# Two key/query buffers instead of four, and the second gate product ahead of the scores

## The chip, the cores and the metric

One core of one Trainium2 chip runs the whole kernel. The metric is the device time of one execution in microseconds (us). A profiled execution shows what TensorE (PE, with its weight loads as PEld), VectorE (DVE), ScalarE (ACT), GpSimd (POOL) and SyncE (SP, which only issues transfers) did and when.

## The reference, cut to what matters

A gated linear attention over 4 batches of 8 heads, 768 steps, head size 40, and behind it a mixture of 8 experts with the best two per token. The attention keeps a matrix `C` and a vector `n` per head and step:

```python
for t in range(S):
    m_new = np.maximum(f_gate[:, :, t] + m, i_gate[:, :, t])
    f_stab = np.exp(f_gate[:, :, t] + m - m_new)
    i_stab = np.exp(i_gate[:, :, t] - m_new)
    C = f_stab * C + i_stab * outer(v, k)
    n = f_stab * n + i_stab * k
    y[:, :, t] = sigmoid(o_gate) * (C @ q) / max(abs(n @ q), 1)
```

The expert part turns the 3072 tokens of 320 features into logits, picks two experts per token, and adds `relu(x @ w1[e]) @ w2[e]` with the two weights.

## The kernel before

The attention is cut into 24 units: two pairs of batches times 12 chunks of 64 steps, each unit with all 8 heads. Inside a unit the steps are handled as a 64 x 64 product per head. A unit u passes through these steps:

- `load_unit(u)` (line 154): keys and queries (`"k"`, four transfers into `QK[u % 4]`, line 159) and values with output gates (`"v"`, two transfers into `VKS[u % 4]`, lines 162 and 163), issued on SP.
- `s_part(u)` (line 333): the scores, 32 small products of keys and queries (line 342), and for all units but the first of a pair 8 products that copy the queries below them (line 339), into PSUM tile `s`, which has two buffers.
- `e_part(u, p)` (line 312): for each half p one matmul of the gate terms `LE` and `RE` into PSUM tile `e` (line 318), which has one buffer, and ScalarE's exponential of it into `W[u]` (line 321).
- `k_part(u)` and `p_part(u)`: VectorE multiplies keys by gate factors (`kd`, line 350) and scores by gate factors (`p`, line 356, or line 360 for the first unit of a pair).
- `c_part(u)`: products into PSUM tile `st` (line 370), the state for the next unit; ScalarE copies it beside the values of u + 1 (line 373).
- `o_part(u)` (line 379): the output products. `f_part(u)`: VectorE divides (lines 384 to 390), POOL multiplies by the gate (`xr`, line 391). `sig_part(u)`: three ScalarE steps make the sigmoid of the output gate.
- `t_part`, `tc_part`, `l_part`, `lc_part`: the output is transposed (line 402), and the router's logits are computed (line 422).

The order on each engine is that of the program text; there is no scheduler. Iteration i of the loop (line 792) emits: transfers for i + 3; `k_part` and `p_part` of i + 1; `c_part` and `o_part` of i; the first half of `e_part(i + 2)`; `f_part(i)`; logits and transposes of i - 1; `s_part(i + 2)`; ScalarE's `sig_part(i + 1)`; the second half of `e_part(i + 2)`; and then pieces of the router's work (`fill`, `act`), which VectorE, ScalarE and POOL do in between. The router ends in bursts of matmuls (line 442) on one-hot tiles `ob` that VectorE makes (line 615).

Rows of `QK` that no transfer fills are cleared once by `blank(i)` (lines 176 to 178), on VectorE or POOL. `keys(i)` (line 246) does the same for `VK`, on POOL. `gate_math` and `gate_move` make the gate terms on VectorE and bring them to `LE` and `RE`.

The pools `att` (with `QK` and `VKS`) and `wk` are closed behind the loop (line 924). The pool `m2` (line 931) of the expert phase takes their place in SBUF: first `RAW2` (10 KB per partition), a filler of `PAD` = 544 words, and then `HH`, the hidden layer, whose first write is at line 992. A tile there waits for the last use of the tiles that it lies over.

Of the kernel before, what the change touches and what calls it, by code (L numbers as in the profile page):

```python
# [7 lines left out]
F32 = mybir.dt.float32  # L8
# [8 lines left out]
B, H, S, D = 4, 8, 768, 40  # L17
# [44 lines left out]
def build(ctx, tc, qk, vk, fi, noise, wgn, w1, w2, cst, ce, out):  # L62
# [39 lines left out]
    HL = gates.tile([64, 2, S], FR, name="hl")  # L102
    es = ExitStack()
    att = es.enter_context(tc.tile_pool(name="att", bufs=1))
    QK = [att.tile([128, 2, H, L], F32, name=f"qk{i}") for i in range(4)]

    VKS = [att.tile([128, 2, VW], F32, name=f"vk{i}") for i in range(4)]
    VK = [[t[:, p, 0:648] for p in range(2)] for t in VKS]
# [45 lines left out]
    def load_unit(u, what="kv", q=None):  # L154
        pr, c = divmod(u, NCH)
        if "k" in what:
            for n in (slice(0, 32), slice(32, D)):
                for p in range(2):
                    (q or SP).dma_start(QK[u % 4][64 * p + n.start:64 * p + n.stop], qk[pr, c, p, n])
        if "v" in what:  # L160
            flat = VKS[u % 4].rearrange("p x c -> p (x c)")
            SP.dma_start(flat[0:64, 0:VW], vk[pr, c, 0])
            SP.dma_start(flat[64:128, 648:648 + VW], vk[pr, c, 1])
# [12 lines left out]
    def blank(i, q):  # L176
        q.memset(QK[i][32:64], 0.0)
        q.memset(QK[i][96:128], 0.0)

# [12 lines left out]
    def run(steps):  # L192
        for _ in steps:
            pass

    def gate_math(t0, t1):
        f, i = fit[:, 0, t0:t1], fit[:, 1, t0:t1]
        n = t1 - t0
        V.tensor_tensor_scan(mt[:, t0 + 1:t1 + 1], f, i, mt[:, t0:t0 + 1], OP.add, OP.max)
        yield  # L200
        gt = gts[t0 // 128 % 2][:, 0:n]
        V.tensor_add(gt, f, mt[:, t0:t1])
        yield
        V.tensor_sub(gt, gt, mt[:, t0 + 1:t1 + 1])
        if t0 == 0:
            V.memset(gt[:, 0:1], 0.0)
        yield
        ag = ags[t0 // 128 % 2][:, :, 0:n]
        V.tensor_tensor_scan(ag[:, 1, :], rmt[:, 0:n], gt, 0.0, OP.mult, OP.add)
        yield  # L210
        V.tensor_sub(ag[:, 0, :], i, mt[:, t0 + 1:t1 + 1])
        yield
        V.tensor_sub(ag[:, 0, :], ag[:, 0, :], ag[:, 1, :])
        yield

        V.tensor_copy(HL[:, :, t0:t1], ag)
        yield
        V.scalar_tensor_tensor(HL[:, :, t0:t1], HL[:, :, t0:t1].bitcast(F32), cet[0:64, E_SG:E_SG + 1], ag, op0=OP.mult, op1=OP.add)
        yield
# [3 lines left out]
    def gate_move(kk, q=(SP, SP)):  # L223
        pr, k = divmod(kk, GB)
        j = kk % 2
        src = HL[32 * pr:32 * pr + 32, :, k * GC * L:(k + 1) * GC * L].bitcast(F32)
        q[0].dma_start(LE[j][64:96, :, 64:128].bitcast(F32), src[:, 0].rearrange("r (c t) -> r c t", c=GC))
        q[1].dma_start(RE[j][96:98].bitcast(F32), src[:, 1])

    def operands(j, p, eng=None):  # L230
        if p is None:
            A.activation(LE[j][0:KE], cet[0:KE, None, E_L:E_L + 192].to_broadcast([KE, GC, 192]), AF.Copy)
        else:
            A.activation(RE[j][0:64, p].rearrange("r h (c t) -> r h c t", c=GC),
                         cet[0:64, None, None, 0:L].to_broadcast([64, H, GC, L]), AF.Copy)

    def heads(j, p, eng):
        o, i = RE[j][64:96, p], cet[64:96, E_H:E_H + H, None].to_broadcast([32, H, GC * L])
        x = cet[64:96, E_P + p:E_P + p + 1]
        if eng is A:  # L240
            A.activation(o, i, AF.Copy, scale=x)
        else:
            V.tensor_scalar(o, i, x, None, op0=OP.mult)


    def keys(i):
        P.memset(VK[i][1][32:64, 0:328], 0.0)
        P.memset(VK[i][0][96:128, 328:648], 0.0)
        P.tensor_copy(VK[i][0][64:104, 328:648].rearrange("p (h d) -> p h d", h=H), ident[64:104, None, 64:104].to_broadcast([40, H, D]))
        P.tensor_copy(VK[i][1][0:64, 328:648].rearrange("p (h d) -> p h d", h=H), ident[0:64, None, 0:D].to_broadcast([64, H, D]))  # L250
# [7 lines left out]
    heads(0, 0, A)  # L258
    heads(0, 1, A)
    load_unit(1, "v")  # L260
    blank(2, P)
    for i in range(2):
        keys(i)
    load_unit(2, "k")
    operands(1, None, A)
    operands(1, 0, A)
    run(gate_math(GC * L, 256))
    gate_move(1)
    heads(1, 0, V)
    gates2 = (s for t0 in (256, 384, 512, 640) for s in gate_math(t0, t0 + 128))  # L270

    def gate_steps(n):
        for _ in range(n):
            next(gates2, None)

    gate_steps(4)
    blank(3, P)
    for i in range(2, 4):
        keys(i)
    load_unit(2, "v")  # L280
    load_unit(3, "k")
    SP.dma_start(fit[:, :, 384:], fi[:, :, 384:])
    SP.dma_start(wgt, wgn)
    def constants():
        P.memset(W1L[0:64, 2].bitcast(F32), 0.0)
        P.memset(zrow, 0.0)
# [44 lines left out]
        SQ[u] = psum.tile([128, 2, 512], F32, name="s", bufs=2).rearrange("p x (h t) -> p x h t", h=H)  # L331

    def s_part(u):
        q = QK[u % 4]
        for h in range(H):
            if whole(u) and h % 4 == 0:
                for p in range(2):
                    r = qrow[p]
                    T.matmul(SQ[u][:, p][r][:, h:h + 4, :], ident[r, r], q[r, 0, h:h + 4, :], start=True, stop=True)
            for p in range(2):  # L340
                r = qrow[p]
                T.matmul(SQ[u][:, p][half[p], h, :], q[r, 1, h, :], q[r, 0, h, :], start=True, stop=True)  # L342
# [102 lines left out]
    def bc_part(t, b, late=False):  # L445
        if b:
            s = late or rt.tile([128, NE * TC], F32, name="share", bufs=2)
            if late:
                V.tensor_add(TBL, TBL, t[:, LGC + 24:LGC + 24 + NE * TC])
            else:  # L450
                A.activation(s, t[:, LGC + 24:LGC + 24 + NE * TC], AF.Copy)
                P.tensor_add(TBL, TBL, s)
            done[0] += len(b[0]) // 2
# [234 lines left out]
    def warm(n):  # L688
        wp = psum.tile([128, 512], F32, name="o")
        for _ in range(n):  # L690
            T.matmul(wp, wz[:, 0:128], wz, start=True, stop=True)
# [3 lines left out]
    s_room(1)  # L695
    s_part(0)
    warm(WARM2)
    e_part(0, first=True)
    s_part(1)
    heads(1, 1, A)  # L700
    e_part(1, first=True)
    operands(1, 1, A)
# [89 lines left out]
    while i < NU - LEAD:  # L792
        unit[0] = i
        spent[0] = 0.0
        while sent:
            SP.dma_start(*sent.pop())
        if 1 <= i and i + 3 < NU:
            load_unit(i + 3)
        if i:
            keep_rows(i - 1)  # L800
        if i % 2 == 0 and i and i // 2 + 2 < 2 * GB:
            gate_move(i // 2 + 2, (P, P) if i < XV else (SP, SP))

        if W1LD <= i < W1LD + 12 and i % 2 == 0:
            j = (i - W1LD) // 2
            piece_w1(0, 512 * (j // 3), j % 3)
        if i == W2AT:
            early_w2(0, 2)
        if i == 3:
            SP.dma_start(cs[:, C_TRI:], cst[:, C_TRI:])  # L810
        if i == 4:
            SP.dma_start(nzt, noise)
        if not begun and done[0] >= E0U[0]:
            decode(0, E0S[1] // 128)
            spent[0] += 0.6
            begun = 1
        if begun and late < len(tiles(0, 0)):
            gather(0, 0, tiles(0, 0)[late:late + 2])
            late += 2
            begun = 2  # L820
        if i == 6:
            constants()
            A.activation(tri, cs[:, C_TRI:C_TRI + 128], AF.Copy)
            A.activation(ones, cs[:, C_ONE:C_ONE + 128], AF.Copy)
            A.activation(iob, cs[:, C_N:C_N + 128], AF.Copy)
        k_part(i + 1)
        p_part(i + 1)
        fill(0.2, False)
        s_room(i + 2)
        c_part(i)  # L830
        o_room(i)
        o_part(i)
        e_part(i + LEAD, (0,))
        if i == 0:
            sig_part(0)
        f_part(i, lambda: fill(0.15, False))
        if i < 2:
            gate_steps(4)
        if i == 0:
            gate_move(2, (P, P))  # L840
        t = l_part(i)
        w = r_part(t)
        b = None if w else b_part(t)
        if i:
            t_part(i - 1)
            tc_part(i - 1)
        lc_part(i, t, w)
        bc_part(t, b)
        s_part(i + 2)
        act()  # L850
        if i:
            sig_part(i + 1)
        e_part(i + LEAD, (1,))
        if i == 0:
            sig_part(1)
        route(i)
        fill((SHARE if i < NU - 3 else 0.8) - spent[0])
        if W1AT <= i < W1AT + 12 and i % 2 == 0:
            next(pre1)
        act()  # L860
        if 0 < i < 7:
            gate_steps(4)
        if 6 <= i < 13:
            P.memset(XG[:, i - 6], 0.0)
        i += 1
# [482 lines left out]
```

## Time and profile before

| what | us |
|---|---|
| three runs | 524.8, 528.34, 535.03 |
| their median | 528.34 |
| the profiled execution | 522.65 |
| its span, first to last instruction | 520.9 |
| mean granted TensorE clock in it | 0.985 of full |

The profiled execution is shorter than the three runs shown. Where the text reads places in the trace, times are us from the start of the span.

### The profile page before, as it was taken

What the parts mean: (1) busy time and instruction counts of PE and PEld (TensorE: products, weight loads), DVE (VectorE), ACT (ScalarE), POOL (GpSimd) and SP (SyncE); (2) the same over time, 40 slices, a digit from 0 to 9 for tenths busy, and PEclk for the clock granted to TensorE, in tenths of its full rate; (3) what the DMA queues carried; (4) which work ended last, traced back from release to release, by engine and by line L of the source; (5) the groups of instructions that cost most, each with busy time, mean ns of one, the idle gap of its engine ahead of it and who ended that gap; (6) DMA issues with size and microseconds to landing.
All of it is one profiled execution on the core that took longest, in us unless ns stands there. A gap on an engine that the chain in (4) does not pass through costs nothing.

```text
span 520.9 us, 13365 instructions
## 1 busy us (share of the span) xinstructions
PE 504.6 (97%) x5130; PEld 473.3 (91%) x5130; DVE 341.3 (66%) x905; ACT 248.7 (48%) x594; POOL 243.3 (47%) x321
## 2 busy tenths in 40 slices
PE   8899999999999999999999999999999999999993
PEld 3788888888889988999999999999999999999993
DVE  6899998986997576763865484377548347546310
ACT  5788879978523255441542354054335325515300
POOL 7545686864543846055415614550562254151033
PEclk9799999999989999999999999999999999999998
DMA  5889999986655848079229516832951683272033
GB/s 153 201 217 243 246 242 248 223 235 207 216 195 165 202 57 213 5 163 234 68 53 274 112 28 139 229 91 48 263 99 51 138 221 88 60 169 26 2 40 41
DMA packets 48955, 76.89 MB, mean 148 GB/s; under 512 B 10645, under 2 KB 37980, under 8 KB 48884
## 3 DMA queue, kind: packets, MB, share of 16 engines
q1 hardware_dynamic: 35668, 52.19, 36.3%
q0 software_dynamic: 11616, 20.57, 20.7%
q10 hardware_dynamic: 1600, 3.21, 2.0%
q8 instruction: 42, 0.69, 0.6%
q14 instruction: 29, 0.24, 0.2%
HBM read 52.42 MB, written 17.40 MB: 134 GB/s over the span
## 4 chain that ended last, share of the span: by engine, by line
PE 66%; DMA 13%; DVE 11%; ACT 3%; issue 2%; POOL 2%; SPq 1%; POOLq 0%; DVEq 0%; ACTq 0%
PE s L981 16%; DMA y_out<-y,tok 9%; PE e L981 8%; PE o L1009 4%; PE o L1008 4%; PE o L1007 4%; PE st L1008 4%; PE st L1009 4%; PE st L1007 4%; PE o L379 4%; PE e L318 3%; PE s L342 2%; DVE hlo L993 2%; PE st L370 2%; DMA qk<-qk_in 2%
## 5 line engine op out<-in xcount | busy, mean ns | idle before, releaser
L1035 POOL DMA_INDIRECT y_out<-y,tok x53 | 87.2, 1645 | 184.8 <-DVE y L1025 182.0
L992 ACT ACTIVATE hh<-s 128x384 fp32r<-128x384 f32 (+3 forms) x91 | 42.6, 470 | 83.8 <-PE s L981 82.7
L981 PE MATMUL s<-xh,w1h 128*128 128x384 f32 (+6 forms) x273 | 76.8, 337 | 0.1
L750 POOL DMA_INDIRECT xg<-rows,tok x53 | 57.3, 1082 | 24.6 <-issue 15.5
L993 DVE SCALAR_TENSOR_TENSOR hlo<-s,hh 128x384 fp32r<-128x384 f32 (+3 forms) x91 | 47.6, 523 | 24.9 <-ACT hh L992 24.3
L981 PE MATMUL s<-xh,w1l 128*128 128x384 f32 (+6 forms) x273 | 61.7, 334 | 0.0
L1009 PE MATMUL o<-w2h,hlo 128*128 128x320 f32 x184 | 56.9, 309 | 0.7 <-DVE hlo L993 0.7
L1008 PE MATMUL o<-w2l,hh 128*128 128x320 f32 x184 | 56.8, 309 | 0.0
L1007 PE MATMUL o<-w2h,hh 128*128 128x320 f32 x184 | 56.3, 306 | 0.2 <-ACT hh L992 0.2
L1009 PE MATMUL st<-w2h,hlo 128*128 128x320 f32 x168 | 51.9, 309 | 0.0
L1008 PE MATMUL st<-w2l,hh 128*128 128x320 f32 x168 | 51.8, 308 | 0.0
L1007 PE MATMUL st<-w2h,hh 128*128 128x320 f32 x168 | 51.2, 305 | 0.0
L981 PEld LDWEIGHTS s<-xh,w1h 128*128 128x128 f32 x273 | 49.2, 188 | 1.5 <-ACT xh L782 0.4
L981 PEld LDWEIGHTS s<-xh,w1l 128*128 128x128 f32 x273 | 47.7, 188 | 1.1 <-DVE xh L784 0.2
L981 PE MATMUL s<-xl,w1h 128*128 128x384 f32 (+6 forms) x182 | 46.1, 334 | 0.3 <-DVE xl L783 0.3
L992 ACT ACTIVATE hh<-e 128x384 fp32r<-128x384 f32 (+3 forms) x45 | 21.3, 473 | 49.3 <-PE e L981 49.3
L981 PE MATMUL e<-xh,w1h 128*128 128x384 f32 (+6 forms) x135 | 38.6, 340 | 0.6 <-DVE hlo L993 0.3
L1025 DVE TENSOR_SCALAR y<-o,gw 128x320 f32<-128x320 f32 x22 | 12.1, 550 | 39.9 <-PE o L1009 39.9
L391 POOL TENSOR_TENSOR xr<-tm,vk 128x320 f32<-128x320 f32 x24 | 21.1, 879 | 34.7 <-DVE tm L390 13.6
L1025 DVE TENSOR_SCALAR y<-st,gw 128x320 f32<-128x320 f32 x20 | 11.0, 550 | 39.3 <-PE st L1009 39.3
L1009 PEld LDWEIGHTS o<-w2h,hlo 128*128 128x128 f32 x184 | 34.5, 188 | 0.9 <-DVE hlo L993 0.9
L1007 PEld LDWEIGHTS o<-w2h,hh 128*128 128x128 f32 x184 | 34.5, 188 | 0.6 <-ACT hh L992 0.4
(237 smaller groups left out, 1290.7 us busy)
## 6 DMA issues: line engine op xcount, KB each, us to landing
vk<-vk_in SPq DMA_DIRECT2D x48, 242.0 KB
raw<-w_in SPq DMA_DIRECT2D x6, 1280.0 KB
raw<-w_in SPq DMA_DIRECT2D x6, 1024.0 KB
qk<-qk_in SPq DMA_DIRECT2D x46, 128.0 KB
y_out<-zrow SPq DMA_DIRECT2D x15, 320.0 KB
raw<-w_in SPq DMA_DIRECT2D x16, 256.0 KB
rows<-xr POOLq DMA_DIRECT2D x23, 160.0 KB, 4.3
xt__2801<-xb SPq DMA_DIRECT2D x40, 72.0 KB
```

The lines of the kernel that those rows point to most:

```text
L318: T.matmul(ps, LE[j][0:KE, c, 64 - 64 * p:192 - 64 * p], RE[j][0:KE, p, :, c * L:c * L + L], start=True, stop=True)
L379: T.matmul(OQ[u][half[p], h, :], PP[u][n, p, h, :], VK[u % 4][p][n, h * 41:h * 41 + 41], start=True, stop=True)
L391: P.tensor_mul(XR[u], tm.rearrange("p h d -> p (h d)"), SG[u % 4])
L750: P.indirect_dma_start(out=XG[0:rows_of(e, t), t], out_offset=None, in_=XD[0:n], in_offset=bass.IndirectOffsetOnAxis(ap=token(e, t), axis= ...
L981: T.matmul(ps[:, 0:n], l, r, start=i == 0, stop=i == len(ops) - 1)
L992: A.activation(hi, x, AF.Relu)
L993: V.scalar_tensor_tensor(lo, x, 0.0, hi.bitcast(F32), op0=OP.max, op1=OP.subtract)
L1007: T.matmul(ps, HH[:, j, c], W2H[:, j], start=j == 0, stop=False)
L1008: T.matmul(ps, HH[:, j, c], W2L[:, j], start=False, stop=False)
L1009: T.matmul(ps, HLO[:, j, c], W2H[:, j], start=False, stop=j == 7)
L1025: V.tensor_scalar(y[0:n], ps[0:n], GW[e][0:n, t:t + 1], None, op0=OP.mult)
L1035: st = P.indirect_dma_start(out=out, out_offset=bass.IndirectOffsetOnAxis(ap=token(e, t), axis=0), in_=y[0:n], in_offset=None, compute_op= ...
```

## The change

`QK` has two buffers instead of four. The two clears of buffers 2 and 3 go. In the loop, the head of iteration i loads only the values of unit i + 3; the keys and queries of unit i + 4 are asked for behind `s_part(i + 2)`, which is the last reader of the buffer that they go into. Ahead of the loop, part of the preparation (gate terms of the second pair of chunks, `keys(2)` and `keys(3)`, loads of units 2 and 3) now stands in the text behind `s_part(0)` and the warm-up matmuls, and the load of unit 3's keys behind `s_part(1)`. From iteration 2 on, the second half of `e_part(i + 2)` stands ahead of `s_part(i + 2)`, and so ahead of `act()` and `sig_part(i + 1)`. In iterations 0 and 1 the order of these is what it was.

```diff
--- before.py
+++ after.py
@@ -102,7 +102,7 @@
     HL = gates.tile([64, 2, S], FR, name="hl")
     es = ExitStack()
     att = es.enter_context(tc.tile_pool(name="att", bufs=1))
-    QK = [att.tile([128, 2, H, L], F32, name=f"qk{i}") for i in range(4)]
+    QK = [att.tile([128, 2, H, L], F32, name=f"qk{i}") for i in range(2)]
 
     VKS = [att.tile([128, 2, VW], F32, name=f"vk{i}") for i in range(4)]
     VK = [[t[:, p, 0:648] for p in range(2)] for t in VKS]
@@ -156,7 +156,7 @@
         if "k" in what:
             for n in (slice(0, 32), slice(32, D)):
                 for p in range(2):
-                    (q or SP).dma_start(QK[u % 4][64 * p + n.start:64 * p + n.stop], qk[pr, c, p, n])
+                    (q or SP).dma_start(QK[u % 2][64 * p + n.start:64 * p + n.stop], qk[pr, c, p, n])
         if "v" in what:
             flat = VKS[u % 4].rearrange("p x c -> p (x c)")
             SP.dma_start(flat[0:64, 0:VW], vk[pr, c, 0])
@@ -258,29 +258,8 @@
     heads(0, 0, A)
     heads(0, 1, A)
     load_unit(1, "v")
-    blank(2, P)
     for i in range(2):
         keys(i)
-    load_unit(2, "k")
-    operands(1, None, A)
-    operands(1, 0, A)
-    run(gate_math(GC * L, 256))
-    gate_move(1)
-    heads(1, 0, V)
-    gates2 = (s for t0 in (256, 384, 512, 640) for s in gate_math(t0, t0 + 128))
-
-    def gate_steps(n):
-        for _ in range(n):
-            next(gates2, None)
-
-    gate_steps(4)
-    blank(3, P)
-    for i in range(2, 4):
-        keys(i)
-    load_unit(2, "v")
-    load_unit(3, "k")
-    SP.dma_start(fit[:, :, 384:], fi[:, :, 384:])
-    SP.dma_start(wgt, wgn)
     def constants():
         P.memset(W1L[0:64, 2].bitcast(F32), 0.0)
         P.memset(zrow, 0.0)
@@ -331,7 +310,7 @@
         SQ[u] = psum.tile([128, 2, 512], F32, name="s", bufs=2).rearrange("p x (h t) -> p x h t", h=H)
 
     def s_part(u):
-        q = QK[u % 4]
+        q = QK[u % 2]
         for h in range(H):
             if whole(u) and h % 4 == 0:
                 for p in range(2):
@@ -695,8 +674,27 @@
     s_room(1)
     s_part(0)
     warm(WARM2)
+    load_unit(2, "k")
+    operands(1, None, A)
+    operands(1, 0, A)
+    run(gate_math(GC * L, 256))
+    gate_move(1)
+    heads(1, 0, V)
+    gates2 = (s for t0 in (256, 384, 512, 640) for s in gate_math(t0, t0 + 128))
+
+    def gate_steps(n):
+        for _ in range(n):
+            next(gates2, None)
+
+    gate_steps(4)
+    for i in range(2, 4):
+        keys(i)
+    load_unit(2, "v")
     e_part(0, first=True)
     s_part(1)
+    load_unit(3, "k")
+    SP.dma_start(fit[:, :, 384:], fi[:, :, 384:])
+    SP.dma_start(wgt, wgn)
     heads(1, 1, A)
     e_part(1, first=True)
     operands(1, 1, A)
@@ -795,7 +793,7 @@
         while sent:
             SP.dma_start(*sent.pop())
         if 1 <= i and i + 3 < NU:
-            load_unit(i + 3)
+            load_unit(i + 3, "v")
         if i:
             keep_rows(i - 1)
         if i % 2 == 0 and i and i // 2 + 2 < 2 * GB:
@@ -846,13 +844,18 @@
             tc_part(i - 1)
         lc_part(i, t, w)
         bc_part(t, b)
+        if i > 1:
+            e_part(i + LEAD, (1,))
         s_part(i + 2)
+        if i + 4 < NU:
+            load_unit(i + 4, "k")
         act()
-        if i:
+        if i == 1:
+            sig_part(2)
+        if i < 2:
+            e_part(i + LEAD, (1,))
+        if i != 1:
             sig_part(i + 1)
-        e_part(i + LEAD, (1,))
-        if i == 0:
-            sig_part(1)
         route(i)
         fill((SHARE if i < NU - 3 else 0.8) - spent[0])
         if W1AT <= i < W1AT + 12 and i % 2 == 0:
```

## Rows read from the trace of the kernel before

**Rows 1.** The page, busy time of the engines: us, share of the span, instructions.
```profile
PE 504.6 (97%) x5130; PEld 473.3 (91%) x5130; DVE 341.3 (66%) x905; ACT 248.7 (48%) x594; POOL 243.3 (47%) x321
```

**Rows 2.** Stretches: length, busy (count) of PE, PEld, DVE, ACT, POOL, clock, DMA, GB/s.
```profile
17.36:25.50 8.14, 8.14 (x139) 6.96 (x140) 6.13 (x13) 5.28 (x12) 3.02 (x6) 0.58 0.95 223
...
22.58:126.06 103.48, 101.80 (x2464) 87.98 (x2464) 90.07 (x233) 87.22 (x215) 66.81 (x104) 0.99 0.94 240
```

**Rows 3.** Chain that ended last, one iteration: start, length in us, what, instructions merged.
```profile
36.97 0.74 PE st L370 x32
...
38.65 0.43 PE e L318
...
40.02 0.21 PE s L339
...
41.12 0.43 PE e L318
41.55 0.75 PE st L370 x32
```

**Rows 4.** Timeline, SP's key issues; PE's gate products that follow scores 4 and 14.
```profile
28.41 2.27 SPq L159 DMA_DIRECT2D qk<-qk_in  x4
...
77.31 2.61 SPq L159 DMA_DIRECT2D qk<-qk_in  x4
...
31.40 0.50 PE L318 MATMUL e<-re,le 98*128 98x512 f32 x1
...
78.99 0.51 PE L318 MATMUL e<-re,le 98*128 98x512 f32 x1
```

**Rows 5.** The chain again: transfers of keys, from issue to landing.
```profile
4.23 2.98 DMA qk<-qk_in
...
50.02 6.82 DMA qk<-qk_in
```

**Rows 6.** Timeline, ScalarE's exponentials of two iterations, and PE's scores at 58.56.
```profile
39.11 0.60 ACT L321 ACTIVATE w<-e 128x512 f32<-128x512 f32 x1 [0.30 <-PE e L318]
...
41.89 0.58 ACT L321 ACTIVATE w<-e 128x512 f32<-128x512 f32 x1
...
58.00 0.58 ACT L321 ACTIVATE w<-e 128x512 f32<-128x512 f32 x1
...
58.56 0.43 PE L339 MATMUL s<-qk,cs 64*64 64x256 f32 x2
```

**Rows 7.** Waits in total: us, times, longest; then who waited for instructions on `qk`.
```profile
DVE kd L350 <- ACT w L321: 5.1, 5, 2.4
...
  PEld s L339: 0.5, 3
```

**Rows 8.** Timeline, the two bursts of rank matmuls, and one wait of VectorE.
```profile
76.47 1.14 PE L442 MATMUL xt<-oa,ob 128*128 128x56 bf16 x12
...
85.35 0.82 DVE L350 TENSOR_TENSOR kd<-vk,w 128x640 f32<-128x640 f32 x1 [1.30 <-ACT w L321]
...
105.41 0.91 PE L442 MATMUL xt<-oa,ob 128*128 128x56 bf16 x12
```

**Rows 9.** Timeline, the start: a clear on POOL, the cast twice, PE's first o.
```profile
11.14 0.95 POOL L178 MEMSET qk<- 32x1024 f32 x1
11.21 1.02 DVE L216 CAST hl<-xg 64x256 fp32r<-64x256 f32 x1
...
17.36 1.92 PE L379 MATMUL o<-vk,p 64*64 64x41 f32 x30 [0.36 <-DVE p L360]
...
28.67 0.28 DVE L216 CAST hl<-xg 64x256 fp32r<-64x256 f32 x1
```

**Rows 10.** Timeline, where the expert phase begins.
```profile
132.07 0.49 ACT L992 ACTIVATE hh<-s 128x384 fp32r<-128x384 f32 x1 [1.00 <-issue]
133.01 0.87 POOL L391 TENSOR_TENSOR xr<-tm,vk 128x320 f32<-128x320 f32 x1 [3.81 <-ACT lg L471]
...
134.67 0.54 DVE L993 SCALAR_TENSOR_TENSOR hlo<-s,hh 128x384 fp32r<-128x384 f32 x1
```

## What the change will do

> **What bounds the kernel now.** I read the page first: TensorE (PE) is busy 97% of the span, VectorE 66%, the rest under half [rows 1]. A busy matrix engine says little of stages with other limits, so the table by stretches comes next. The change touches only the attention loop and what stands ahead of it, so I cut out the stretch from iteration 1's first `st` product to the first transpose of the expert phase: 103.48 us, in which PE is busy 101.80, ScalarE 87.22, VectorE 90.07, and the DMA engines' share is 0.94 [rows 2]. There is 1.68 us of PE idle time in it. The other row of that group shows the one stretch at a low clock: from 17.36 to 25.50 the granted clock is 0.58, most of it the lower level (1.2 GHz). PE had waited for VectorE just before, until 17.36 [rows 9].
>
> Then the chain of work that ended last, in order of time. From about 17 us to 48 us it is PE after PE. One plain iteration reads [rows 3]: `st` products from 36.97, first gate product 38.65, transposes until 40.02, scores from 40.02 to 41.12, second gate product 41.12 to 41.55, where the next one starts. The period is 41.55 - 36.97 = 4.58 us, the scores take 1.10 and a gate product 0.43. Iterations 1 to 21 take 103.48/21 = 4.93 each, so 21 x 0.35 = 7.3 us is all that any change of order inside the loop could give, and part of that is extra work (rank matmuls, low clock).
>
> The list of waits then tells what PE isn't waiting for: keys and queries. All waits on `qk` that PE's weight loads have are 0.5 us in three times. VectorE does wait for the gate factors: 5.1 us in five waits [rows 7].
>
> **The change, part by part.**
>
> *Two query/key buffers.* Nothing is computed less. The load of unit u goes into the buffer that the scores of u-2 read, so its four issues on SyncE (SP) wait for the end of those scores. The order of SP's transfers stays: before, the head of iteration i issued keys of i+3, then values of i+3; now the tail of i issues keys of i+4, and the head of i+1 values of i+4. Only small rows of routing weights change places with them. Behind the new wait stand the values of the same unit, the weight pieces and the constants. The values wait for the POOL product of four units back anyway, which comes at about the same time; who would wait for them is `kd`, most of an iteration after the last of the scores in question.
>
> How much later is the issue? Before, keys of unit 16 were asked for at 77.31; the scores of 14 end at 78.99, and with the gate product ahead of them 0.43 later, at 79.42: 2.1 us later. Keys of unit 6: 28.41 against 31.40 + 0.43, 3.4 us later, about the worst of all [rows 4]. It matters only if the data come after PE wants them. From the end of scores u-2 to the start of scores u there are two periods less one score block: 2 x 4.58 - 1.10 = 8.06 us; the 0.43 moves both ends and drops out. Issuing four takes up to 2.61 us [rows 4]. Issue to landing of one such piece is 2.98 us at the start and 6.82 us in the crowded middle [rows 5]; the trace gives no others, so these are the bounds. Together at most 2.61 + 6.82 = 9.43, at least 1.7 (four issues of the median length, estimated from the shorter groups) + 2.98 = 4.7. But the row of 6.82 us belongs to the second of its four, not the last, and waiting on SP overlaps with a queue that is still draining; 1.7 + 5 = 6.7 is nearer to the middle. So I take 0 us. The upper bound: if every unit took 9.43, a period would be (9.43 + 1.10)/2 = 5.27 instead of 4.58; with the 4.93 of now that is 0.34 x 21 = 7 us.
>
> The Trainium skill (DMA: Bandwidth & Descriptors, Anatomy of one DMA) says that a semaphore wait happens on the issuing sequencer before dispatch, and its Rules for kernel authors say to issue a DMA early and wait late. This speaks against the change: a load behind a wait holds up all SP issues behind it. By that rule alone the sum would be the upper bound, +7; by the rows, with a lead of 8.06 us, 0.
>
> *The second gate product ahead of the scores, from iteration 2.* No instruction is added. PE: the product must wait until ScalarE has emptied the only `e` bank, which the first product filled. ScalarE's exponential ran 39.11 to 39.71, and PE reaches the place at 40.02, 0.3 us after. In tight iterations it ran 58.00 to 58.58 and PE arrives at 58.56 [rows 6]. Three or four iterations are like that (where extra ScalarE work stands ahead); at about 0.1 us each: +0.3, between 0 and, if half of the iterations lost 0.15 us, +1.5. ScalarE: the second exponential goes from 41.89 [rows 6] to right behind its product, about 40.02 + 0.43 + 0.1 = 40.55; the three sigmoid steps go behind it, the sum is the same. VectorE: gate factors come 1.3 us earlier, scores 0.43 later; `kd` (0.82) stands ahead of `p` and covers that 0.43. So its waits of 5.1 us mostly go away. But `kd` and `p` are made one iteration ahead of their use on PE, so PE gains only where VectorE has fallen behind by that much: the bursts of rank matmuls wait for one-hot tiles, 1.14 us at 76.47 and 0.91 us at 105.41 for the same 12 matmuls [rows 8]. The second stands behind a VectorE that has hardly paused since the wait of 1.30 us at 85.35. Bounds: nothing, or all that exceeds a free burst of some 0.5 us, that is 0.6 + 0.4 = 1.0. I take -0.5.
>
> *The start.* Apart from the loads, the moved lines pass only PE's own work (warm-up, scores), so VectorE's and ScalarE's order does not change. The load of unit 3 waits for the scores of unit 1, long done by then. Two clears of 2 x 0.95 us on POOL (buffers 2 and 3) disappear. The later pair stands beside VectorE's critical work: the cast at 11.21 took 1.02 us, ending 0.14 us behind a clear that ended at 12.09; the same cast without it took 0.28 us at 28.67 [rows 9]. That cast lies on the way to `p` of unit 0, for which PE waits at 17.36. Between 0 (other POOL work slides into its place) and -0.74; POOL's next operations are shorter clears, so I take -0.5. The Trainium skill (SBUF — State Buffer, Who interferes with whom) says that a VectorE cast in a two-port mode and a GpSimd operation exclude each other for the whole instruction, whichever starts first. By it all of the 0.74 comes back if POOL is quiet there (a sum of 521.9) and none if another of its operations stands in the same place (522.6); my value gives 522.1.
>
> *The memory that comes free.* 2 x 4 KB per partition move all later tiles of that pool down by 8 KB. The hidden-layer tile `hh` (from 12.4 KB into the pool) then lies over the last of the four value buffers. Its first write, at 132.07, would have to wait for the last gating product on POOL, 133.01 + 0.87 = 133.88 [rows 10]: 1.8 us on ScalarE. VectorE uses that result only at 134.67, so the 0.49 us activation still ends in time. 0 to +1.8; I take +0.2.
>
> **Sum.** 0 + 0.3 - 0.5 - 0.5 + 0.2 = -0.5 us on the profiled execution of 522.65 us (span 520.9, 1.75 us around it): 522.1. The three runs shown have a median of 528.34, 5.7 us above that execution, and spread from 524.8 to 535.03. I take the change over as a difference: 528.3 - 0.5 = 527.8.
>
> **Rivals.**
>
> *Keys come late; the slow side.* One mechanism: the transfer outlasts the lead. It costs from 8.06 us on. At the bounds of the rows, 9.43, it is +7 (535). For 2% (10.5 us) the period must grow by 0.5 to 5.43, so issue to landing must reach 2 x 5.43 - 1.10 = 9.76 us in every unit. For it: DMA share 0.94, and one piece at 6.82. Against it: the delays come out of a queue that is full, so a later issue mostly means less time in the queue. Late within 2% (+4 to +10, taken as 534): 0.11; over 2% (at least 539): 0.08.
>
> *The clock does not fall at the start.* If PE's pause before 17.36 gets shorter, the stretch 17.36 to 25.50 may run at the higher level throughout: 8.14 x (1 - 0.58) = 3.4 us less, 524.4 with the sum. For it: the pause ends 0.5 us sooner. Against it: most of the pause stays. 0.11, within 2%.
>
> *The loop closes up.* All 7.3 us of excess and the 3.4 us of clock would be 517.6, just 2%. Rank matmuls and pauses inside the score blocks are not touched by the change, so this needs more than it does: 0.05.
>
> *The new order does nothing:* factors were early enough anyway. That is my forecast less 0.5: the same case.
>
> **How the numbers follow.** Forecast 0.65, plus late within 2% 0.11 and clock 0.11: 0.87 for no change within 2%, about what a measurement of this kernel can tell from none. Faster by more 0.05, slower by more 0.08. The range reaches to the clock rival and the lowest execution seen below (522), and to the late keys above (535): 13 in 100 stay outside.
>
> **What would show it.** Right: the plain iteration still takes 4.58 us, with gate product ahead of scores; `kd` waits for `w` well under 5.1 us; key issues on SP start at the end of the scores two units back; cast near 11.2 us under 0.6; first `hh` behind the last `xr`. Wrong: PE's score blocks waiting for `qk`; SP issues further and further behind; a second stretch at the low clock; PE waiting at the second gate product for `w` in most iterations.

## The result and the profile after

The changed kernel took 1.0101 [1.0069, 1.0133] of the time of the kernel before, measured beside it (medians 532.54 and 527.77 us). Beside the last experiments, on another chip, it took 1.0039 [1.0000, 1.0078]. So it is slower: by one per cent in the first comparison, by 0.4% in the second, whose interval just touches no change. That is within the 2% that most of my chance lay on, but on the other side of nothing than my forecast of -0.5 us. The mechanism that makes it slower was none of my rivals. The profiled execution of after has a span of 525.5 us, 4.7 more than before; each of the two profiled executions is as short as the shortest run of its kernel in the first comparison, or shorter.

The page, engine by engine (busy us, share of the span, instructions), and the queue that brings TensorE's own instructions (packets, MB, share of 16 DMA engines):

```profile
PE 499.7 (95%) x5130; PEld 471.0 (90%) x5130; DVE 343.3 (65%) x905; ACT 248.4 (47%) x594; POOL 239.1 (45%) x317
...
q8 instruction: 42, 0.69, 0.6%
```

Against [rows 1] PE is 4.9 us less busy in a span that is 4.7 us longer: PE idles more. The last line was on the page of before too, and I had passed over it. It turns out to matter.

Two stretches of after, with the columns of [rows 2]:

```profile
16.84:24.77 7.93, 7.68 (x213) 6.41 (x215) 7.65 (x15) 6.76 (x16) 3.17 (x5) 1.00 0.95 226
29.60:36.50 6.90, 6.90 (x115) 6.35 (x113) 4.79 (x10) 3.83 (x9) 1.52 (x2) 0.51 0.41 116
```

The start runs at the full clock, where [rows 2] had 0.58; but a stretch at the lower level follows at 29.6, which before did not have, and which the prediction had named as a sign of being wrong. What stands between them is in the chain that ended last (start, length, what):

```profile
21.60 0.43 PE e L297
22.03 0.34 PE xt L381 x3
...
22.41 0.79 POOL le L227
23.20 5.89 DMA re<-hl
29.09 0.14 issue
29.23 0.47 PE e L297
```

PE waits 3.35 us for the gate terms of unit 4, whose transfer POOL asks for at 23.20. Up to o(2), the output products of unit 2, after is 3.1 us ahead; at o(3) it is 2.25 us behind. The two in after, then the two in before:

```profile
24.77 1.10 PE L358 MATMUL o<-vk,p 128*64 128x41 f32 x32
34.84 1.84 PE L358 MATMUL o<-vk,p 128*64 128x41 f32 x32
...
27.90 1.10 PE L379 MATMUL o<-vk,p 128*64 128x41 f32 x32
32.59 1.48 PE L379 MATMUL o<-vk,p 104*64 104x41 f32 x32
```

From 25 to 135 us, who waited for what (total, times, longest):

```profile
PE o L358 <- issue: 1.9, 2, 0.9
PE s L321 <- issue: 0.5, 1, 0.5
...
PEld s L318 <- DMA qk<-qk_in: 0.7, 2, 0.4
...
DVE kd L329 <- ACT w L300: 2.0, 2, 1.5
```

Keys are as little waited for as in [rows 7]. VectorE's wait for gate factors fell from 5.1 to 2.0 us, as forecast. New is the first line: PE stops inside the output products, and nothing that the profile knows holds it ("issue"). Such stops as such are not new: before had two in the scores, in the same stretch, which I had not asked about:

```profile
PE s L342 <- issue: 1.0, 2, 0.6
```

Where the loss lies is easiest read from two times of each profile: the start of the last gating product `xr` on POOL, the end of the attention, and the rest of the span.

| kernel | last `xr` starts | rest of the span |
|---|---|---|
| before | 133.01 | 387.8 |
| after | 136.43 | 389.1 |
| after, second profile | 138.78 | 394.2 |
| new order alone | 140.99 | 387.9 |
| two buffers, old order | 130.82 | 387.9 |

The rest, three quarters of the kernel, differs little by the change. (It is 391 to 395 us in all kernels of the later two groups of runs, which were on other chips; the second profile of after is from there.) Most of the loss of after, 3.4 of 4.7 us, and all of the loss with the new order alone are made ahead of the last `xr`. Single executions scatter, and some profiled ones are among the longest of their kernels (the second of after, and below the gate terms on SP, the shifted old order and the later clears with gate terms on SP); two of these have the old order and start their last `xr` at 138.83 and 136.11, as late as the new order. So one profile does not tell the orders apart, and the verdicts below rest on the ratios.

### The profile page after: what moved, and what is told of

Same layout as the page of the kernel before. It is cut to its first block, busy times and chain, and to the rows that moved or that the text cites. A ratio compares the mean times of both kernels' runs of the same rounds, so it can differ in the third digit from the quotient of the medians.

```text
span 525.5 us, 13351 instructions
## 1 busy us (share of the span) xinstructions
PE 499.7 (95%) x5130; PEld 471.0 (90%) x5130; DVE 343.3 (65%) x905; ACT 248.4 (47%) x594; POOL 239.1 (45%) x317
## 4 chain that ended last, share of the span: by engine, by line
PE 59%; DVE 13%; DMA 13%; ACT 7%; issue 4%; POOL 2%; SPq 1%; POOLq 0%; ACTq 0%; DVEq 0%
PE s L984 15%; DMA y_out<-y,tok 9%; PE e L984 8%; PE o L1012 4%; PE o L1011 4%; PE o L1010 4%; PE st L1012 4%; PE st L1011 4%; PE st L1010 4%; PE o L358 2%; DVE hlo L996 2%; PE e L297 2%; DVE ob L594 2%; PE s L321 2%; PE st L349 2%
```

## The experiments

**One part at a time.** After the two traces I put three theories on record. A: the start runs ahead and then waits for the gate terms. B: the new order itself costs, by PE waiting for ScalarE's exponential. C: keys asked for late cost. None of them names those stops of PE. Four kernels on one chip, beside the kernel before (median 522.72).

New order alone, in the kernel before:

```diff
+        if i > 1:
+            e_part(i + LEAD, (1,))
         s_part(i + 2)
         act()
...
+        if i < 2:
+            e_part(i + LEAD, (1,))
...
-        e_part(i + LEAD, (1,))
```

> The kernel before with one part of the change alone: from iteration 2 on the second gate product stands ahead of the scores; four key/query buffers, loads and start as before. Theory A (the start runs ahead and then waits for the gate terms of units 4 and 5, sent by POOL's queue): the start is that of before, so PE's low clock near 17 to 24 us and no wait of 3 us for re<-hl; plain iterations shorten from 4.58 to about 4.4 us as in the changed kernel; time 0.99 to 1.00 of before. Rival B (the new order itself costs, by PE waiting for the exponential): 1.005 to 1.01. Rival C (two buffers, late keys): 1.00.

Measured: 527.90, ratio 1.0066 [1.0029, 1.0103]. That is slower, where A expected 0.99 to 1.00, and has the size of B. B's cause is not in the trace: from 25 to 135 us PE's weight loads wait 0.7 us in all for the exponential, its products not at all.

Two buffers alone: the changed kernel with these lines put back as they were.

> The changed kernel with the order of second gate product and scores put back: two buffers, late key loads and the moved start remain. Theory A: as the changed kernel at the start (no low clock before 25 us, then 3 us of waiting for re<-hl at 26 to 29 us, low clock behind it), plain iterations of 4.58 us; 1.01 to 1.015 of before. Rival B (order): 1.00. Rival C (late keys): 1.01, with waits of PE's weight loads on qk of several us in all.

Measured: 522.10, ratio 0.9979 [0.9949, 1.0009]. Without the new order nothing is lost: neither A (1.01 to 1.015) nor C (1.01) is borne out, and two buffers, the later issue of keys and the moved start cost nothing that the measurement can tell. The order alone costs 0.66%, the whole change 1.01% and 0.39% on two other chips, so whether the order is all of its loss is not shown.

Clears later: in the kernel before, the second pair of clears on POOL goes behind `keys(2)` and `keys(3)`.

```diff
-    blank(3, P)
     for i in range(2, 4):
         keys(i)
+    blank(3, P)
```

> The kernel before with the clear of buffer 3 on POOL moved behind the four keys() blocks, nothing else. Theory A: the cast near 11.2 us takes well under 1.0 us, PE's first output products start some 0.5 us earlier than 17.36, and if the clock then stays up PE waits for re<-hl near 26 to 28 us: 1.00 to 1.005 of before. Rivals B and C: 1.00 and the start as before.

Measured: 521.91, ratio 0.9969 [0.9932, 1.0006]. The start is as A expected: the cast takes 0.43 us, PE's `o` starts at 16.61, the clock is full from 17 to 28 us, and PE waits 1.54 us for the gate terms of unit 4. But the clock stays behind that wait, and the kernel is not slower. Whether and where the clock falls in the first 40 us differs between profiles of kernels with the same start (17.6 to 24.4 with two buffers alone, 29.6 to 36.5 in after); nothing in these traces decides it.

Gate terms on SP: in the changed kernel the transfers of the gate terms of units 4 and 5 go through SP's queue.

```diff
-            gate_move(2, (P, P))
+            gate_move(2, (SP, SP))
```

> The changed kernel with the gate terms of units 4 and 5 sent through SP's queue, ahead of the keys of unit 4, instead of POOL's. Theory A: they land near 26 us instead of 29.1, the wait of 3.35 us shrinks below 1 us, no low clock behind it: 4 to 5 us less than the changed kernel, 1.00 of before or a little under. Rivals B and C: no difference to the changed kernel, 1.01.

Measured: 525.68, ratio 1.0046 [1.0013, 1.0079], where A expected 1.00 or a little under. The gate terms are asked for at 21.61, `e` of unit 4 runs at 25.79 without the wait, and the loss stands elsewhere: three stops inside the output products make 5.6 us, and the clock falls behind two of them. Waits of PE between 25 and 135 us, and the clock (column as above) in the stretches behind two stops:

```profile
PE o L358 <- issue: 5.6, 3, 3.1
...
42.70:49.70 7.00, 7.00 (x105) 6.27 (x105) 5.81 (x10) 3.85 (x11) 3.75 (x6) 0.51 0.57 170
97.40:104.20 6.80, 6.80 (x96) 6.07 (x98) 4.72 (x22) 3.27 (x9) 3.27 (x7) 0.50 0.42 123
```

**What the stops are.** In the run with the new order alone they are larger than in after (waits of PE from 25 to 135 us, then the longest on the timeline):

```profile
PE o L379 <- issue: 5.1, 4, 2.3
PE o L379 <- DVE tm L390: 1.4, 3, 0.6
PE s L342 <- issue: 0.9, 1, 0.9
PE s L339 <- issue: 0.8, 2, 0.4
...
97.49 0.31 PE L379 MATMUL o<-vk,p 104*64 104x41 f32 x3 [2.30 <-issue]
```

PE halts between the 29th and the 30th of 32 equal products on the same tiles, and the profile shows no wait for a tile there. Counting instructions up to each stop tells more. Stretches from 0 to just ahead of four of the stops; the counts (x) of PE and PEld are what to read:

```profile
0.00:35.06 35.06, 28.98 (x467) 20.52 (x469) 28.95 (x64) 25.07 (x43) 20.66 (x42) 0.85 0.79 184
0.00:40.30 40.30, 33.92 (x593) 24.99 (x595) 33.31 (x73) 28.32 (x51) 22.60 (x45) 0.87 0.81 193
...
0.00:59.36 59.36, 51.74 (x970) 40.68 (x972) 47.21 (x101) 42.78 (x87) 32.32 (x62) 0.88 0.84 203
0.00:97.48 97.48, 86.60 (x1849) 71.64 (x1850) 80.76 (x197) 74.09 (x165) 58.55 (x103) 0.93 0.87 212
```

Products and weight loads together: 936, 1188, 1942, 3699. The steps are 252, 754 and 1757, that is 1, 3 and 7 times 251 to 252. With the records of PE's sequencer (its waits and branches) counted too, a step is 256, within two. The queue q8 of the profile's page brings instructions in packets of 16 KB (0.69 MB in 42), and 42 x 256 = 10,752 is a little over the 10,401 records of PE in this profile. So the stops are at boundaries of PE's own instruction pages. The other profiles agree. Over all fourteen, from 17 us to the last `xr`, 31 stops of more than 0.25 us that nothing releases have the same place in the count of 256 (192 to 194); all others belong to one group between 111 and 121 us, of 0.3 to 0.5 us each. The stretch around the longest stop shows the packet missing (DMA queues: packets, MB, share), first from the boundary before it, 90.2, to 94.85, then from 94.85 to 96.5:

```profile
q1 hardware_dynamic: 367, 0.95, 76.0%
q0 software_dynamic: 126, 0.30, 19.3%
q14 instruction: 1, 0.01, 0.6%
```
```profile
q1 hardware_dynamic: 169, 0.42, 94.6%
q0 software_dynamic: 42, 0.02, 6.0%
q8 instruction: 1, 0.02, 4.5%
```

Behind each boundary one packet follows. PE crosses one at 90.2; the packet starts only at 94.9, 4.7 us later, while data fill the queues, and PE, halted at the next boundary, goes on at 97.49, 2.6 us behind that start. Over all stops here it goes on 2.3 to 3.1 us after its page's packet starts. With the new order alone the packet starts 2.55 us behind the boundary on average (18 boundaries from 25 to 130 us, ten of them over 2.5), with the old order 1.87 (19, five over 2.5).

A page lasts PE about one iteration, mostly 4.6 to 5.5 us, so by these numbers a delay of more than some 2 to 3 us uses up the time. No stop came behind a delay under 2.6 us; of the delays over 2.5, seven of ten ended in a stop with the new order, two of five with the old. These are two profiles: over all with full loads the averages are 1.4 to 2.45 us with the old order (six) and 2.0 to 2.8 with the new (five), so they overlap; the stops at boundaries sum to 0 to 1.8 us and to 2.4 to 6.8, and do not.

Behind the stop of 2.30 us the clock falls:

```profile
97.50:99.60 2.10, 2.10 (x24) 1.77 (x28) 1.72 (x17) 0.98 (x2) 0.67 (x1) 1.00 0.99 254
99.60:103.00 3.40, 3.40 (x88) 3.28 (x80) 2.84 (x6) 2.59 (x9) 2.60 (x7) 0.50 0.65 171
```

The Trainium skill (Runtime: NRT & Kernel Launch, Instruction fetch mechanics) says that a sequencer fetches its instructions in 16 KiB blocks of 256 through a DMA queue of its own, and that the cost of crossing a boundary is mostly hidden. This trace agrees with 256. Mostly hidden fits before, where two boundaries halted PE; with the new order alone seven did, one for 2.30 us.

**Load or order, and place.** Theory: the pages come late because data fill the DMA engines, and the new order only asks faster. Rivals: the order is slower by itself; or it matters only where in an iteration the boundary falls. Four kernels on a second chip (before there 529.72). The two light kernels load half of the rows of the values from unit 4 on; the other rows keep what an earlier unit left, so the output is not the reference's:

```diff
-            SP.dma_start(flat[0:64, 0:VW], vk[pr, c, 0])
-            SP.dma_start(flat[64:128, 648:648 + VW], vk[pr, c, 1])
+            n = 64 if u < 4 else 32
+            SP.dma_start(flat[0:n, 0:VW], vk[pr, c, 0, 0:n])
+            SP.dma_start(flat[64:64 + n, 648:648 + VW], vk[pr, c, 1, 0:n])
```

> The kernel before, with the loads of the values of units 4 to 23 cut to half of their rows (the other rows keep the values of an earlier unit, so the output is not the reference's; the instructions of the engines are the same). A control for the next run. Late-pages theory (the order costs because the loop then asks for its work faster, the 16 DMA engines fill up, and the 16 KB pages of TensorE's own instructions land late): DMA share of the loop falls from 0.94 to 0.70 to 0.80, TensorE's stalls with no other releaser than issue fall from 1.0 us to under 0.5, time 0.985 to 1.000 of before. Order theory (the new order is itself slower, whatever the DMA does): the same here, since the order is the old one.

> The kernel before with the new order of the second product of gate factors alone, and the loads of the values cut to half of their rows as in the run above (output not the reference's). Late-pages theory: the stalls named issue, 6.8 us in the run with full loads, fall under 1 us, the clock stays as in the control, and the time against the control is 0.992 to 1.000 (the run with full loads stands at 1.007). Order theory: it stays 1.005 to 1.010 of the control. VectorE as bound: 0.998 to 1.002 of the control.

Measured: old order 0.9991 [0.9956, 1.0026] of before, new order 0.9969 [0.9927, 1.0011]. The DMA share from 25 to 126 us fell from 0.94 to 0.64 and, with the new order, from 0.88 to 0.66. The new order's waits of PE at light load:

```profile
PE st L371 <- issue: 1.4, 3, 0.5
PE o L380 <- DVE tm L391: 1.1, 3, 0.7
PE s L343 <- issue: 0.8, 1, 0.8
...
PE xt L423 <- issue: 0.6, 1, 0.6
```

Two stops at boundaries are left, 0.8 and 0.6 (under 1 us in all was expected), of seven that summed to 6.8. (The three of 0.5 at `st` near 113 us are at no boundary and stand in most traces, after's too; I have no cause for them.) The intervals of the two light kernels overlap, so at light load no cost of the order is left to see. On the same chip the new order with full loads (shifted, below) is 1.0055 [1.0014, 1.0096], clear of the light 0.9969 [0.9927, 1.0011].

The shifted kernels have 126 more instructions ahead of the loop, for the same columns:

```diff
-            T.matmul(wp, wz[:, 0:128], wz, start=True, stop=True)
+            for k in range(cut):
+                x = slice(k * 512 // cut, (k + 1) * 512 // cut)
+                T.matmul(wp[:, x], wz[:, 0:128], wz[:, x], start=True, stop=True)
...
-    warm(WARM)
+    warm(WARM, 4)
...
-    warm(WARM2)
+    warm(5, 4)
+    warm(WARM2 - 5)
```

> The kernel before, with 21 of the 28 warm-up products cut into four of a quarter of the columns: 126 more TensorE instructions of the same total columns ahead of the loop, so that the boundaries of TensorE's instruction pages fall half an iteration away from where they fell. Late-pages theory: old order leaves the fetches time wherever the boundary falls, stalls named issue 0 to 1.5 us, time 0.997 to 1.003 of before. Place theory (it is only where the boundary falls in an iteration that decides, and the old order had luck): stalls of 3 us or more, 1.003 to 1.010.

> The new order alone with the same 126 instructions ahead. Late-pages theory: the stalls move to other instructions and other iterations, but their sum stays 3 to 8 us and the time 1.003 to 1.010 of before. Place theory: the stalls fall to 0 to 1.5 us and the time to 0.996 to 1.002.

Measured: old order 1.0017 [0.9961, 1.0072], new order 1.0055 [1.0014, 1.0096]. The stops of the new order, shifted, sum to 3.8 us at four boundaries (old order 1.8 at two, a little over the 1.5 expected). Stretches up to the first two:

```profile
0.00:62.05 62.05, 56.34 (x1222) 48.73 (x1223) 54.77 (x117) 48.16 (x102) 34.95 (x65) 0.94 0.85 213
0.00:68.60 68.60, 61.28 (x1348) 53.15 (x1349) 59.56 (x140) 52.98 (x114) 40.70 (x76) 0.95 0.86 216
```

2445 and 2697: 2 and 3 steps of 251.5 behind the 1942 of above. The stops stayed on the same grid of counts while the work under it moved by half an iteration, and they hit other iterations. That shows that they belong to the instruction pages and not to a piece of work. The place rival is not borne out (new order shifted is still above 1), though the interval of the shifted old order is wide.

**The change at light load, and two versions that might have won.** Four kernels on a third chip (before there 528.78).

> The changed kernel, with the loads of the values of units 4 to 23 cut to half of their rows (output not the reference's). Late-pages theory: stalls named issue at the page boundaries under 1.5 us, and what is left of the loss is the start's (wait for the gate terms and a clock that falls behind it, 2.25 us of 528): 0.998 to 1.004 of before, 0.993 to 0.998 of the changed kernel with full loads. Rival (order or buffers themselves cost): within 0.2% of the changed kernel.

> The changed kernel once more, beside the others on the same chip and with a second profile. Late-pages theory: stalls named issue of 2 to 7 us at the page boundaries in the loop, 1.005 to 1.012 of before.

Measured: the changed kernel 1.0039 [1.0000, 1.0078], with halved value loads 0.9958 [0.9923, 0.9992]. The two intervals do not touch. All three figures lie a little below the expected ones: 1.0039 (1.005 to 1.012), 0.9958 (0.998 to 1.004), and their quotient 0.992 (0.993 to 0.998). At full load the stops of PE repeat after's, the same boundaries halt (3448, 3699 and 5206 instructions; in after 3449, 3700 and 5207), and the clock falls behind the first (0.50 from 87.3 to 90.7) and behind the second and larger one:

```profile
93.64 0.31 PE L358 MATMUL o<-vk,p 104*64 104x41 f32 x3 [1.77 <-issue]
...
94.10:101.00 6.90, 6.90 (x109) 6.24 (x110) 4.59 (x22) 3.92 (x10) 3.27 (x7) 0.51 0.46 139
```

At light load the same products run through, and no boundary halts in the whole loop:

```profile
92.02 1.10 PE L359 MATMUL o<-vk,p 128*64 128x41 f32 x32
93.06 0.50 PE L298 MATMUL e<-re,le 98*128 98x512 f32 x1
```

In these profiles the last `xr` starts at 132.74 us, in the light kernel with the old order at 133.18; at full load it was 138.78 and, in the profile of before, 133.01. At light load the packets start 1.15 us behind the boundary on average. The wait for the gate terms is no shorter there (1.8 us against 1.4 at full load), so that wait is not what the light loads took away. From o(3) to o(16) the changed light kernel takes 92.02 - 32.08 = 59.94 us, the light kernel with the old order, on the second chip, 92.92 - 31.48 = 61.44: 1.5 us less in 13 iterations. The new order alone at light load takes 92.97 - 31.68 = 61.29, with one stop of 0.57 at a boundary in it, so it is not shown that the order is worth 1.5.

Two versions with the old order and gate terms on SP, the one with two buffers, the other with four and the later clears:

> The changed kernel with the order of the second product put back, and the gate terms of units 4 and 5 moved by SP's queue and not by POOL's. Late-pages theory: no order, so no late pages (stalls named issue under 1.5 us); where the clock does not fall at the start, the head start of some 3 us at o(2) is not lost to a wait for the gate terms: 0.993 to 0.998 of before, against 0.998 of the same kernel with POOL's queue. Rival (the queue of the gate terms is worth nothing): 0.997 to 1.001.

> The kernel before with the second pair of clears behind the raising of its keys on POOL, and the gate terms of units 4 and 5 on SP's queue: no second buffer pair less, no new order. If the start is all there is to win: the 1.5 us wait for the gate terms in the run with the clears alone goes, 0.992 to 0.997. If not: 0.996 to 1.001, as the clears alone.

Measured: 1.0006 [0.9966, 1.0047] and 0.9981 [0.9949, 1.0014]. The expected 0.5% was not there: both are the kernel before, within the intervals. In the first, the clock fell from 17.4 to 27.6 us in the profiled execution, so there was no head start to keep. No version tried with full loads beats the kernel before by more than the measurement can tell.

## Why the prediction was wrong

**The place of the loss: wrong.** The step that failed is the second gate product ahead of the scores: +0.3 for PE waiting and -0.5 for bursts, bounds -1.0 and +1.5. Alone it measured 1.0066, about +3.5 us of 522.7, outside the bounds. Both terms were about right as far as they went. In after PE waits for ScalarE at that product 0.2 us in all. The two bursts of 12 rank matmuls take 0.76 and 0.47 us where [rows 8] had 1.14 and 0.91, 0.8 less together. What the sum lacked, put at nothing without a reason, is a term for a resource that was on the page in one line: PE's own instruction pages, on DMA engines that [rows 2] shows 0.94 busy. Their stops were 1.0 of the 1.68 us of idle time that I read in before, and sum to 6.8 us in the profile of the new order alone. I used the 0.94 only to ask how long keys take.

**The plain iteration: wrong in the other direction.** I wrote that it stays at 4.58 us. It became 4.38 to 4.40 (output products at 39.96, 44.34, 48.74). Most of the gain lies behind the transposes: from the start of the last three to the next product it is 0.45 us before (44.09 to 44.54, scores next) and 0.29 in after (46.30 to 46.59, gate product next). The gate product itself costs nearly the same in both places: 0.44 us behind the scores (45.63 to 46.07) and 0.41 ahead of them (46.59 to 47.00). Iterations of 4.38 to 4.40 us stand in every profile of the new order; by my reading, which no run separates, this gain also brings PE to its page boundaries sooner.

**Keys late, the slow rival: refuted.** PE's weight loads wait 0.7 us in all for keys, and two buffers alone are 0.9979. My choice of 0 between 0 and +7 was right. So the lead of 8.06 us covers the later issue here. (One reading of mine was off: issuing four takes up to 2.91 us in before, not 2.61; nothing came of it.) The rule of the Trainium skill (DMA: Bandwidth & Descriptors, Rules for kernel authors) on issuing early, which I had put beside it, did not decide.

**The start: right in size, incomplete in its end.** PE's first `o` starts at 16.84, not 17.36: the -0.5 of the sum. The cast beside the clears takes 0.53 (timeline of after), where [rows 9] had 1.02:

```profile
10.90 0.53 DVE L216 CAST hl<-xg 64x256 fp32r<-64x256 f32 x1
10.92 0.36 POOL L247 MEMSET vk<- 32x328 f32 x1
```

The rival that the clock does not fall came true in this execution, but not for the reason given: PE's pause ahead of `o` is 0.36 us as in [rows 9]. Start and clock, priced at 0.5 and 3.4, gave 3.1 us together. I did not ask what is late next: PE then comes to the gate terms of unit 4, whose transfer had just been in time before (landed at 28.14, wanted at 28.93), waits 3.35 us, and the clock falls behind that wait. So 3.1 us of gain became 2.25 of loss at o(3). In this one profile the wait is more than the stops at boundaries, 2.4 us in all.

**The memory that comes free: right.** The first `hh` waits for the last `xr`, as I said, and costs nothing: from `xr` to the first `hlo` it is 1.43 us (136.43 to 137.86), before 1.66 [rows 10].

```profile
136.43 0.87 POOL L370 TENSOR_TENSOR xr<-tm,vk 128x320 f32<-128x320 f32 x1 [3.81 <-DVE mx L503]
...
137.33 0.49 ACT L995 ACTIVATE hh<-s 128x384 fp32r<-128x384 f32 x1 [2.83 <-POOL xr L370]
```

**What the loss is made of.** The stretch from 17 us to the last `xr`, in before, with the new order alone, and in after (columns as in [rows 2]):

```profile
17.00:133.01 116.01, 113.97 (x2612) 98.64 (x2612) 100.76 (x267) 95.32 (x236) 69.19 (x111) 0.97 0.88 226
17.00:140.99 123.99, 115.39 (x2609) 101.75 (x2606) 101.09 (x266) 95.38 (x235) 68.35 (x106) 0.93 0.84 211
17.00:136.43 119.43, 110.22 (x2611) 97.88 (x2610) 102.47 (x266) 93.74 (x232) 67.89 (x106) 0.97 0.84 219
```

PE is idle for 2.0, 8.6 and 9.2 us. The clock is at its lower level for 6.8, 17.1 and 6.8 us, and half of that is lost. What is left, PE's work at the full clock, is 110.6, 106.9 and 106.8 us. So by this reckoning the new order saves some 3.7 us of work, as the shorter iterations say, and loses more than that: alone by 6.6 us more of idle time (5.8 of it at page boundaries) and 5.1 us of clock, 1.7 of that at the start and ahead of any stop; in after by 7.2 us of idle time, most of it the wait for the gate terms and the stops.

**What stays open.** The runs show that the stops are at instruction page boundaries, that they come with the new order and go with half of the value loads, and that the loss with the new order goes with them. They do not show why the new order delays the packets more than the old one at a DMA share that is no higher (0.94 old, 0.87 to 0.88 new over the loop, stops included). Nor do they show, beyond single profiles, what part of the loss is PE's stops and what the clock that falls behind them: the mean granted clock is 0.982 in the runs with the new order alone and 0.989 in the runs of before beside them, and 0.7% of 522 us is 3.7 us, but 3.7 us of work saved have to be lost as well. That is a comparison and not an experiment; no run held the clock or removed the stops alone.

## What to carry to other kernels

In a loop that keeps the DMA engines busy, an engine that executes hundreds of instructions per iteration has its own instructions to fetch through them, and a stop with no releaser should be checked against the instruction count. A gain on PE of a few tenths of a microsecond per iteration was worth nothing here while such a fetch had no slack, and a stop can cost more than its length if the granted clock falls behind it. When a part ahead gets faster, ask which transfer had been just in time.

## What the runs showed of the hardware that I had not expected

A boundary of 256 instructions halted PE for up to 3.1 us (at 97.35 with the gate terms on SP), though the 42 packets that bring the pages are 0.6% of the DMA engines' time. Halving one load, 0.94 to 0.64 of DMA share, took the old order nowhere (0.9991), and the changed kernel from 1.0039 to 0.9958. Behind stops and waits of PE the granted clock often went to its lower level for 3.4 to 7 us (3.35 us of wait at 29.23 in after, 1.77 at 93.64 in its second profile, 2.30 at 97.49 with the new order alone), once for 13.7 us (2.04 at 27.95 in the shifted old order), and sometimes not (1.54 at 27.19 with the later clears, 1.61 at 68.61 in the shifted new order): the length of the stop alone did not decide.
